# First attention of a three-stage kernel: masks added by quarters of the array, routing products padded to the whole array, first w1 loaded in four steps

## The chip, the cores and the metric

The kernel runs on one core of a Trainium2 chip. The metric is the device time of one execution in microseconds. Each execution works on the whole input: four batches of 576 tokens.

## The reference, cut to what matters

Three layers follow one another: an attention with fixed masks, a mixture of eight experts with one expert per token, and a mixture of four attention experts with two per token.

```
def _attn_ref(q, k, v):                      # q, k, v: (4, 8, 576, 64)
    scores = scale * q @ k.T
    rel = pos[:, None] - pos[None, :]
    mask_local = (rel >= 0) & (rel < 32)                     # heads 0 to 3
    mask_strided = (rel >= 0) & (pos[None, :] % 32 == pos[:, None] % 32)   # heads 4 to 7
    scores = where(mask, scores, -1e9); softmax; @ v
def _moe_ref(x, w_gate, w_local, w1, w2):    # 8 experts, D 512, F 1024
    for each batch b, token s in order:
        fresh = argmax(logits[b, s])
        e = fresh if s == 0 or sigmoid(x @ w_local) < 0.5 else previous token's e
        out[b, s] = softmax(logits)[e] * (relu(x @ w1[e]) @ w2[e])
def _moe2_ref(x, ...):                       # 4 experts, each a causal attention, the top 2 added
```

The output is the third layer's, (4, 576, 512) in float32. The change touches the first layer and the choice of the expert (the routing) in the second.

## The kernel before, in words

The program has one instruction list per engine, and the first about 125 us of it are the first attention. That attention is cut into 16 units, four to a batch: units 0 and 1 of a batch (`u < LOC`) hold two heads each with the local mask, units 2 and 3 two heads each with the strided mask. A unit goes through these functions: `prep` (L342) turns q and k around with transposes on PE, ScalarE (ACT) moves them out of PSUM; `s_mm` (L369 to L393) makes the scores in the PSUM tile `s`, of which there is one; `et` (L405, L409, L416) transposes the weights after the exponential; `pv` (L428, L447) multiplies by v; POOL's queue writes the result to memory (`xd`); `xt` (L469, L472, L476) transposes it again for the routing.

In `s_mm` the mask comes first: for each of the two heads `h` one product of a 128x128 identity in bf16 (`idb`) with a table of zeros and -1e30 (`ml` for local, `ms` for strided) writes the bank of that head with 384, 480 or 288 columns (L369). The scores are then added to it by products that use a quarter of the array each: rows 64h to 64h+63 by the head, columns 64g to 64g+63 by the half of the output's partitions (L374 for local, 64x96; L382 for strided, 36x36, whose outputs start at partitions 0 and 64).

```
for h in range(2):
    nc.tensor.matmul(p[:, h, :nb * w], idb, m, start=True, stop=False, skip_group_check=True)
```

The routing of a batch is a chain of small steps between the units: `logits` (L490), `route0`, `route1` (L507, L508: two transposes that give the logits by token, the second of 32 rows), `route_w`, `route2` (L546: two products with the five columns of `r_key` as the weights), `route2b` (L555, L556: two products with the five rows of `r_row`), `route3` (L571 to L578: ranks, the last product with the one row of `bump`), `route3b` (L613, L619), `route_r`, `route4` (L636: the slots of the tokens).

The order of the work is written out by hand. Each function call is an event with a time; the list is sorted by time and then called in the order of the table `ORD` (309 events). PE runs in exactly the order of the calls (`manual_schedule`); for the other engines the scheduler of the framework places the instructions, so their order also depends on the calls. All loads stand in one queue, SyncE's (SP), in order; a load whose buffer is still read waits there, and so does everything behind it.

Beside the attention the first expert is made ready. `load_w1(0)` is one event that issues four loads of 512 KB (L162) into four buffers called `w1raw`; `split_w1` (16 events, called from `ORD`) splits each buffer in four parts into a rounded part on ACT (L118, `w1h`) and a rest on VectorE (DVE, L119, `w1l`). `load_w2e` (L176) then takes the same four buffers for `w2`, and `split_w2e` splits that. After about 125 us come `xt_early`, `h_early` and `y_early` (expert 0 on the rows of the first three batches), then experts 1 to 7 with their weights streaming in, then the third layer from about 400 us.

Before the units PE does 24 products with zeros (`warm`, L714).

Of the kernel before, what the change touches and what calls it, by code (L numbers as in the profile page):

```python
# [11 lines left out]
BF = mybir.dt.bfloat16  # L12
I32 = mybir.dt.int32
AF = mybir.ActivationFunctionType
OP = mybir.AluOpType
# [17 lines left out]
ORD = [5, 2, 0, 4, 7, 1, 3, 8, 10, 6, 11, 16, 12, 22, 19, 14, 20, 13, 17, 9, 18, 21, 24, 25, 26, 23, 29, 27, 15, 31,  # L33
# [12 lines left out]
NORM = [[[0, 1], [0, 0]], [[1, 0], [0, 0]], [[0, 1], [0, 0]], [[0, 1], [0, 0]], [[0, 0], [1, 1]]]  # L46
# [10 lines left out]
def kernel(  # L57
# [100 lines left out]

    def load_w1(e):
        for c in range(4):  # L160
            t = wpool.tile([128, F], FT, name="w1raw", bufs=4)
            nc.sync.dma_start(t, moe_w1[e, c * 128:(c + 1) * 128, :])  # L162
            RAW1[e, c] = t
# [95 lines left out]
    es = [slot(3, [128, 2, 4, 128], FT, "es0"), ak.tile([128, 2, 5, 128], FT, name="es1")]  # L259
    ml = ac.tile([128, 6, 96], BF)  # L260
    ms = ac.tile([128, 8, 36], BF)
# [8 lines left out]
    for x in kl:  # L270
        nc.vector.memset(x[:, :32], 0.0)
    nc.vector.tensor_copy(ml, ml1[:, None, :].to_broadcast([128, 6, 96]))
    nc.vector.memset(ml[:64, 1, :32], NEG)
    for x in vl:
# [87 lines left out]
    def s_mm(n):  # L362
        b, u = divmod(n, NU)
        loc = u < LOC
        nb, w = (4 + u, 96) if loc else (8, 36)
        p = pa.tile([128, 2, 512], FT, name="s", tag="s", bufs=1)
        m = (ml[:, 1 - u:5] if loc else ms).rearrange("p c k -> p (c k)")
        for h in range(2):
            nc.tensor.matmul(p[:, h, :nb * w], idb, m, start=True, stop=False, skip_group_check=True)  # L369
        if loc:  # L370
            for c, g, a, t in tiles(u):
                for h in range(2):
                    r = slice(64 * h, 64 * h + 64)
# [125 lines left out]
    slot_acc = ac.tile([128, RC, 6, NE], FT)  # L499
    bump = cst.tile([1, NE], BF)  # L500
    lim = cst.tile([128, 2], FT)
    nc.vector.memset(bump, 0.0)

    def route1(b):
        lg = lgs[b % 2]
        p = bank([128, NC5, 32], "lgt")
        nc.tensor.transpose(p[:, :4].rearrange("p g e -> p (g e)"), lts[:, :128], idf)  # L507
        nc.tensor.transpose(p[:, 4], lts[:32, 128:], idf[:32, :32])  # L508
        nc.vector.tensor_copy(lg, p[:, :, :9])
        l8 = lg[:, :, 1:]  # L510
# [10 lines left out]
        nc.vector.scalar_tensor_tensor(fr, lg[:, :, 0], ZC, first, op0=OP.is_lt, op1=OP.max)  # L521
        key = rt.tile([128, 2, NC5], BF, name="r_key", bufs=1)
        nc.vector.tensor_tensor(key[:, 0], m8, fr, op=OP.mult)
        nc.vector.tensor_scalar(key[:, 1], fr, -1.0, 1.0, op0=OP.mult, op1=OP.add)
        ex = rt.tile([128, NC5, NE], FT, name="r_ex", bufs=1)
        nc.vector.tensor_tensor(ex, l8, mxb, op=OP.subtract)
        nc.scalar.activation(ex, ex, AF.Exp)
        RT[b] = key
        EX[b] = ex
# [11 lines left out]
    def route2(b):  # L541
        key = RT[b]
        row = rt.tile([NC5, 128], BF, name="r_row", bufs=1)
        p = bank([NC5, 2, 128], "kr")
        for n in (1, 0):
            nc.tensor.matmul(p[:, n], key[:, n], idb, start=True, stop=True)  # L546
        nf = rt.tile([NC5, 128], FT, name="r_nf", bufs=1)
        nc.scalar.activation(nf, p[:, 1], AF.Copy)
        nc.vector.tensor_tensor_scan(row, nf, p[:, 0], 0.0, op0=OP.mult, op1=OP.add)
        RT[b] = row  # L550

    def route2b(b):
        row = RT.pop(b)
        p = bank([128, 2, NC5], "pk")
        nc.tensor.matmul(p[:, 0], row, idb[:NC5, :NC5], start=True, stop=True)  # L555
        nc.tensor.matmul(p[:, 1], row[:, 127:].to_broadcast([NC5, 128]), idb[:NC5, :NC5], start=True, stop=True)  # L556
        un = rt.tile([128, 2, NC5], FT, name="r_un", bufs=1)
        nc.vector.tensor_scalar(un[:, 0], p[:, 1], 0.0, None, op0=OP.is_equal)
        nc.vector.tensor_tensor_scan(carry[:, 1:], un[:, 0], p[:, 1], 0.0, op0=OP.mult, op1=OP.add)
        nc.vector.scalar_tensor_tensor(un[:, 1], p[:, 0], 0.0, carry[:, :NC5], op0=OP.is_equal, op1=OP.mult)  # L560
        pk = rt.tile([128, NC5], FT, name="r_pk", bufs=1)
        nc.vector.tensor_tensor(pk, un[:, 1], p[:, 0], op=OP.add)
        PK[b] = pk

    def route3(b):
# [11 lines left out]
        if b:  # L577
            nc.tensor.matmul(pr, ones_b[:1], bump[:1, None, :].to_broadcast([1, NC5, NE]), start=False, stop=True,  # L578
                             skip_group_check=True)
# [30 lines left out]
    def route3b(b):  # L610
# [5 lines left out]
        if b == B - 2:  # L616

            pn = bank([1, 1], "pn")
            nc.tensor.matmul(pn, ones_b[:, :1], ohs[:, :1], start=True, stop=True)  # L619
            bm = rt.tile([1, 1], FT, name="r_bm", bufs=1)  # L620
            nc.vector.tensor_scalar(bm, pn, -1.0, float(EARLY), op0=OP.mult, op1=OP.add)
            nc.vector.tensor_scalar(bump[:, :1], bm, 0.0, None, op0=OP.max)

# [59 lines left out]
    def count():  # L683
        p = bank([128, NE], "cnt")
        nc.tensor.matmul(p, ones_b, ohs, start=True, stop=False, skip_group_check=True)
        nc.tensor.matmul(p, ones_b[:1], bump, start=False, stop=True, skip_group_check=True)
        nc.vector.tensor_copy(ext, p)
# [58 lines left out]
    for b in range(B):  # L746
# [4 lines left out]
        ev += [(o + x, *y) for x, y in zip(t, r)]  # L751
    ev += [(SL[0], slots, (slice(0, 2), slice(0, 1), lambda: gather(0, [0, 1], (B - 1) * S))), (6, load_w1, (0,))]
    for c in range(4):
# [698 lines left out]
```

## Time and profile before, and how to read it

| what | us |
|---|---|
| three timed executions | 586.32, 593.21, 592.51 |
| their median | 592.51 |
| the profiled execution, whole | 586.57 |
| its span (first to last instruction) | 584.8 |

The profile comes from one execution. It names engines: PE is the matrix engine, PEld its weight loads, DVE VectorE, ACT ScalarE, POOL GpSimd, SP SyncE; SPq is the queue of loads. A line such as L369 is a line of the kernel before. In the timeline each row is a run of equal instructions: the start in us from the span's start, the time from the first's start to the last's end, the engine and line, what is written from what, the weights' rows and columns (128*128), the moving operand, and the count. Brackets give the idle time ahead of it and what ended it; "issue" stands where the profile shows nothing that the engine waited for. The shares of the DMA are of 16 engines; q8 and q14 of the DMA queues bring instructions.

### The profile page before, as it was taken

To read this page: it belongs to the slowest core of one execution; us is meant where nothing else is said; L and a number is where in the kernel's file an instruction comes from. 1 tells how busy PE (TensorE), PEld (TensorE's weight loads), DVE (VectorE), ACT (ScalarE), POOL (GpSimd) and SP (SyncE) were. 2 spreads that over 40 slices of the span, in tenths; PEclk is the share of its full clock that TensorE was granted. 3 is DMA by queue.
4 is the path that set the end of the run, shared out by engine and by line. 5 is a ranking of instruction groups with operands and counts; after the bars stand their busy time and mean duration, and the time that the engine had idled before them with its cause. 6 is when DMAs were issued, how large, how long until landed. Compare 5 with 4: busy or idle time off the path is not lost. (4 is left out here: it accounts for less than half of the span.)

```text
span 584.8 us, 14159 instructions
## 1 busy us (share of the span) xinstructions
PE 554.6 (95%) x5217; PEld 478.5 (82%) x5217; DVE 383.4 (66%) x1138; ACT 345.9 (59%) x864; POOL 148.8 (25%) x239
## 2 busy tenths in 40 slices
PE   7889899969999999999999999998999999999996
PEld 3778687758779898988989987797987998889864
DVE  2446789855583646474747476158998889898891
ACT  2466775741274544564646567345877876776882
POOL 8232313250422432423343443220000001000000
PEclk9699899989999999999999999999999999999999
DMA  9999989640485765275747360325003402301302
GB/s 182 185 223 217 266 205 218 209 151 1 132 302 191 224 211 167 87 218 192 259 132 251 132 203 28 102 78 129 26 19 71 157 2 58 96 20 41 114 20 90
DMA packets 81127, 82.01 MB, mean 140 GB/s; under 512 B 56840, under 2 KB 57096, under 8 KB 80528
## 3 DMA queue, kind: packets, MB, share of 16 engines
q1 hardware_dynamic: 72768, 64.92, 40.2%
q0 software_dynamic: 8112, 15.76, 8.4%
q8 instruction: 59, 0.97, 0.7%
q14 instruction: 28, 0.23, 0.1%
q10 hardware_dynamic: 160, 0.13, 0.1%
HBM read 61.89 MB, written 21.76 MB: 143 GB/s over the span
## 5 line engine op out<-in xcount | busy, mean ns | idle before, releaser
L196 POOL DMA_INDIRECT yd<-y,sidx x47 | 51.2, 1089 | 91.5 <-ACT y L971 54.3
L1272 ACT ACTIVATE E<-cs,c_mx 128x288 f32<-128x288 f32 (+4 forms) x96 | 45.8, 482 | 13.7 <-DVE c_mx L1270 6.5
L122 PE MATMUL yp<-w2h,h 128*128 128x512 f32 x128 | 51.1, 399 | 0.1
L124 PE MATMUL yp<-w2h,h 128*128 128x512 f32 x128 | 49.9, 390 | 0.0
L123 PE MATMUL yp<-w2l,h 128*128 128x512 f32 x128 | 49.9, 390 | 0.0
L119 DVE TENSOR_TENSOR w1l<-w1raw,w1h 128x1024 fp32r<-128x1024 f32 (+1 forms) x44 | 41.5, 981 | 12.6 <-ACT w1h L118 12.6
L119 DVE TENSOR_TENSOR w2l<-w2raw,w2h 128x512 fp32r<-128x512 f32 x56 | 35.7, 686 | 19.3 <-ACT w2h L118 18.8
L1302 POOL MEMSET E<- 128x128 f32 x40 | 8.3, 211 | 145.7 <-PE cet L1321 68.6
L118 ACT ACTIVATE w1h<-w1raw 128x1024 fp32r<-128x1024 f32 (+1 forms) x44 | 33.9, 837 | 18.6 <-PE hp L123 18.6
L118 ACT ACTIVATE w2h<-w2raw 128x512 fp32r<-128x512 f32 x56 | 31.8, 631 | 18.9 <-PE yp L124 8.2
L705 DVE SCALAR_TENSOR_TENSOR h<-hp,h 128x384 fp32r<-128x384 f32 x48 | 24.8, 552 | 27.2 <-ACT h L704 27.0
L1265 PE MATMUL cs<-qkt 128*128 128x288 f32 (+4 forms) x192 | 39.1, 319 | 0.4 <-DVE qkt L1195 0.4
L1270 DVE TENSOR_REDUCE c_mx<-cs 128x1 f32<-128x288 f32 (+4 forms) x80 | 37.8, 484 | 1.7 <-PE cs L1265 1.0
L122 PE MATMUL qkp<-y,cw 128*128 128x288 f32 x128 | 38.7, 303 | 0.0
L124 PE MATMUL qkp<-y,cw 128*128 128x288 f32 x128 | 37.7, 295 | 0.0
L123 PE MATMUL qkp<-y,cw 128*128 128x288 f32 x128 | 37.7, 294 | 0.0
L704 ACT ACTIVATE h<-hp 128x384 fp32r<-128x384 f32 x48 | 21.4, 490 | 19.6 <-PE hp L124 19.5
L190 POOL DMA_INDIRECT xg<-xd,gidx x24 | 25.1, 1047 | 27.9 <-DVE gidx L648 20.9
L122 PE MATMUL hp<-xo,w1h 128*128 128x320 f32 (+2 forms) x96 | 30.4, 317 | 0.1
L1316 PE MATMUL cet<-idf,E 128*128 128x128 f32 x160 | 28.2, 278 | 2.4 <-ACT et L115 0.8
L123 PE MATMUL hp<-xo,w1h 128*128 128x320 f32 (+2 forms) x96 | 30.1, 314 | 0.0
L124 PE MATMUL hp<-xo,w1l 128*128 128x320 f32 (+2 forms) x96 | 30.1, 314 | 0.0
(371 smaller groups left out, 1683.8 us busy)
## 6 DMA issues: line engine op xcount, KB each, us to landing
w1raw<-in_moe_w_dram SPq DMA_DIRECT2D x32, 512.0 KB
w2raw<-in_moe_w_dram SPq DMA_DIRECT2D x56, 256.0 KB
qkt<-qkt SPq DMA_DIRECT2D x8, 576.0 KB
yr<-yd SPq DMA_DIRECT2D x16, 256.0 KB
out_dram<-co SPq DMA_DIRECT2D x16, 256.0 KB
raw<-in_q_dram SPq DMA_DIRECT2D x16, 144.0 KB
raw<-in_k_dram SPq DMA_DIRECT2D x16, 144.0 KB
raw<-in_q_dram SPq DMA_DIRECT2D x8, 288.0 KB
```

What stands on the lines that cost most here:

```text
L118: nc.scalar.activation(hi, src, AF.Copy)
L119: (eng or nc.vector).tensor_tensor(lo, src, hi.bitcast(FT), op=OP.subtract)
L122: nc.tensor.matmul(o, ah, bh, start=start, stop=False, **kw)
L123: nc.tensor.matmul(o, ah, bl, start=False, stop=False, **kw)
L124: nc.tensor.matmul(o, al, bh, start=False, stop=stop, **kw)
L190: nc.gpsimd.indirect_dma_start(out=t, out_offset=None, in_=xd[:rows], in_offset=bass.IndirectOffsetOnAxis(ap=gidx[:, r, e:e + 1], axis=0))
L196: nc.gpsimd.indirect_dma_start(out=yds[n], out_offset=bass.IndirectOffsetOnAxis(ap=ix(n), axis=0), in_=y, in_offset=None, bounds_check=yds ...
L705: nc.vector.scalar_tensor_tensor(lo, p, 0.0, hi.bitcast(FT), op0=OP.max, op1=OP.subtract)
L1265: nc.tensor.matmul(o[:, h - h0], T[:, h, q0:q0 + 128], T[:, 2 + 2 * x + h, k0:k1], start=x == 0, stop=x == 1, skip_group_check=True)
L1270: nc.vector.tensor_reduce(mx[:, n, h0:h0 + G], o, axis=AX.X, op=OP.max, negate=True)
L1272: nc.scalar.activation(E[:, h, k0:k1], o[:, h - h0], AF.Exp, bias=mx[:, n, h:h + 1], accum_out=sm[:, n, h:h + 1])
L1316: nc.tensor.transpose(p[:, kt * 128:kt * 128 + 128], E[:, kt * 128:kt * 128 + 128], idf)
```

## The change

Three things, and the order table that goes with them. First, `s_mm` adds each mask by four products instead of two: identity rows and columns 64 by 64, rows by the head, columns by the half of the output's partitions, which are the quarters that the score products use; the table of the local mask becomes one block longer (`ml` 7 instead of 6 blocks, 128x672), so that both halves of the partitions can take their own window of it. Second, the routing's small products get whole operands: the second transposition of the logits takes 128 rows of `lts` instead of 32, `key` and `row` become fixed tiles of 128 columns and 128 rows that POOL clears once, `bump` has 128 rows, `pn` 128 outputs. Third, `load_w1(0)` is four events, one for each 512 KB, each with its own place in `ORD`.

```
 def load_w1(e):  ->  def load_w1(e, cs=range(4)):   # for c in cs
-    ml = ac.tile([128, 6, 96], BF)
+    ml = ac.tile([128, 7, 96], BF)
-    nc.vector.memset(ml[:64, 1, :32], NEG)
+    nc.vector.memset(ml[:, 1, :32], NEG)
-        m = (ml[:, 1 - u:5] if loc else ms).rearrange("p c k -> p (c k)")
         for h in range(2):
-            nc.tensor.matmul(p[:, h, :nb * w], idb, m, start=True, stop=False, skip_group_check=True)
+            r = slice(64 * h, 64 * h + 64)
+            for g in range(2):
+                m = (ml[r, 2:6 + u] if g else ml[r, 1 - u:5]) if loc else ms[r]
+                nc.tensor.matmul(p[64 * g:64 * g + 64, h, :nb * w], idb[r, r], m.rearrange("p c k -> p (c k)"),
+                                 start=True, stop=False, skip_group_check=True)
-    bump = cst.tile([1, NE], BF)
+    bump = cst.tile([128, NE], BF)
+    key = ac.tile([128, 2, 128], BF)
+    row = ac.tile([128, 128], BF)
+    nc.gpsimd.memset(key, 0.0)
+    nc.gpsimd.memset(row, 0.0)
-        nc.tensor.transpose(p[:, 4], lts[:32, 128:], idf[:32, :32])
+        nc.tensor.transpose(p[:, 4:].rearrange("p g e -> p (g e)"), lts[:, 128:], idf)
-        nc.tensor.matmul(p[:, 0], row, idb[:NC5, :NC5], start=True, stop=True)
+        nc.tensor.matmul(p[:, 0], row, idb[:, :NC5], start=True, stop=True)
-            nc.tensor.matmul(pr, ones_b[:1], bump[:1, None, :].to_broadcast([1, NC5, NE]), ...
+            nc.tensor.matmul(pr, ones_b, bump[:, None, :].to_broadcast([128, NC5, NE]), ...
-            pn = bank([1, 1], "pn")
+            pn = bank([128, 1], "pn")
-    ev += [..., (6, load_w1, (0,))]
+    ev += [(6 + c * .01, load_w1, (0, (c,))) for c in range(4)]
-    63, 64, 48, 67, 65, 37, 35, 36, 77, 74, 72, 69, 70, 49, 71, 55, 66, 78, 81, 62, 61, 83, 84, 87, 68, 95, 90, 73,
+    63, 64, 48, 67, 65, 37, 35, 36, 77, 74, 72, 69, 70, 49, 71, 55, 66, 78, 81, 62, 61, 83, 84, 87, 68, 98, 93, 73,
...
```

On PE, in the routing of the third batch and the first strided unit behind it (`lgt` is the routing's transposition, `s` the scores' tile, `ms` the strided mask, `kr` the product with the key), before:

```order
566 L507 MATMUL lgt<-idf,lts 128x128
567 L508 MATMUL lgt<-idf,lts 128x32
568 L369 LDWEIGHTS idb
569 L369 MATMUL s<-ms,idb 128x288
570 L369 LDWEIGHTS idb
571 L369 MATMUL s<-ms,idb 128x288
572 L382 MATMUL s<-ks_122,qs_120 36x36 x32
573 L546 LDWEIGHTS r_key
574 L546 MATMUL kr<-idb,r_key 5x128
```

And the same place of the changed kernel on PE:

```order
622 L514 MATMUL lgt<-idf,lts 128x128
623 L515 MATMUL lgt<-idf,lts 128x128
624 L371 LDWEIGHTS idb
625 L371 MATMUL s<-ms,idb 64x288
626 L371 LDWEIGHTS idb
627 L371 MATMUL s<-ms,idb 64x288
628 L371 LDWEIGHTS idb
629 L371 MATMUL s<-ms,idb 64x288
630 L371 LDWEIGHTS idb
631 L371 MATMUL s<-ms,idb 64x288
632 L385 MATMUL s<-ks_122,qs_120 36x36 x32
633 L549 LDWEIGHTS key
```

Nothing changes places on PE; two mask products become four, and each is as long as before.

In SP's queue, where the first expert's w1 is loaded (the loads of q and k are `raw`, those of v are `vla`, `vlb`, `vl` for the local and `vs` for the strided heads), the difference:

```order
 L230 DMA raw_102<-in_k_dram 72x2x512
-L162 DMA w1raw<-in_moe_w_dram 128x1024 x4
+L162 DMA w1raw<-in_moe_w_dram 128x1024
 L240 DMA vla<-in_v_dram 64x4x64
 L240 DMA vlb<-in_v_dram 96x4x64
...
 L240 DMA vlb<-in_v_dram 96x4x64
+L162 DMA w1raw<-in_moe_w_dram 128x1024
 L228 DMA raw_100<-in_q_dram 96x6x64 x2
 L228 DMA raw_100<-in_k_dram 96x6x64 x2
```

One chunk stays where four were; the second stands behind the nine loads of v that follow, the third and fourth further behind, among the loads of the fourth batch.

On ACT, where w1 is split, before and then after:

```order
73 L353 ACTIVATE qs_120<-prep 128x288
74 L118 ACTIVATE w1h<-w1raw 128x256 x8
75 L353 ACTIVATE qs_120<-prep 128x288
76 L115 ACTIVATE ess<-et 128x400
77 L115 ACTIVATE kl_119<-prep 128x288
78 L353 ACTIVATE ql_117<-prep 128x288
79 L118 ACTIVATE w1h<-w1raw 128x256
```

```order
84 L115 ACTIVATE xT_128<-xt 128x512
85 L115 ACTIVATE xT_129<-xt 128x8x36
86 L115 ACTIVATE es_132<-et 96x512
87 L118 ACTIVATE w1h<-w1raw 128x256 x4
88 L115 ACTIVATE xT_129<-xt 128x8x36
89 L115 ACTIVATE ks_123<-prep 128x288
90 L115 ACTIVATE xT_129<-xt 128x8x36
91 L115 ACTIVATE es_132<-et 96x512
92 L396 ACTIVATE z_127<-z_127 128x960
```

At row 74 four splits remain of the eight, and the second chunk's four stand at row 87, where before the last six of the sixteen stood.

## Rows read from the trace of the kernel before

**Rows 1.** The page, busy time of the engines and the granted clock in 40 slices.

```profile
PE 554.6 (95%) x5217; PEld 478.5 (82%) x5217; DVE 383.4 (66%) x1138; ACT 345.9 (59%) x864; POOL 148.8 (25%) x239
PEclk9699899989999999999999999999999999999999
```

**Rows 2.** Stages: busy PE, PEld, DVE, ACT, POOL (count each), clock, DMA share, GB/s.

```profile
0.00:125.00 125.00, 109.84 (x2333) 87.85 (x2333) 82.01 (x257) 75.10 (x179) 48.53 (x104) 0.95 0.87 208
...
250.00:400.00 150.00, 149.13 (x899) 132.07 (x899) 82.63 (x143) 81.27 (x145) 51.55 (x53) 1.00 0.49 157
```

**Rows 3.** Timeline of PE, 58 to 69 us.

```profile
59.05 0.34 PE L447 MATMUL pv<-vs,ess 64*64 64x65 f32 x7
61.65 0.57 PE L447 MATMUL pv<-vs,ess 64*36 64x65 f32 x25 [2.25 <-issue]
62.15 1.23 PE L342 MATMUL prep<-idf,raw 96*128 96x96 f32 x14
```

**Rows 4.** Timeline of PE around 38 and 102 us.

```profile
37.84 0.31 PE L447 MATMUL pv<-vs,ess 64*64 64x65 f32 x4 [1.04 <-issue]
...
102.23 0.41 PE L490 MATMUL lg<-xT,wg 128*32 128x128 f32 x5 [0.68 <-issue]
```

**Rows 5.** PE's products counted between those waits (columns: busy, count, clock, DMA).

```profile
37.83:61.64 23.81, 21.55 (x505) 1.00 0.90 221
61.64:102.22 40.58, 39.08 (x888) 0.96 0.92 226
```

**Rows 6.** DMA queues, 52.5 to 58.5 us, then the instruction queue, 58.5 to 61.5 us.

```profile
q1 hardware_dynamic: 697, 1.33, 84.4%
q0 software_dynamic: 79, 0.26, 12.3%
q14 instruction: 1, 0.01, 0.3%
...
q8 instruction: 1, 0.02, 2.7%
```

**Rows 7.** PE in two stretches of low clock (columns: busy, count, clock, DMA).

```profile
16.00:26.10 10.10, 8.89 (x108) 0.50 1.02 176
63.70:67.10 3.40, 3.40 (x65) 0.50 1.07 266
```

**Rows 8.** Timeline of SP's queue.

```profile
52.74 2.74 SPq L162 DMA_DIRECT2D w1raw<-in_moe_w_dram  x4
...
68.22 0.48 SPq L240 DMA_DIRECT2D vlb<-in_v_dram  x1
...
91.27 1.32 SPq L176 DMA_DIRECT2D w2e<-in_moe_w_dram  x1
```

**Rows 9.** Timeline of ACT, 63 to 99 us.

```profile
63.86 2.56 ACT L118 ACTIVATE w1h<-w1raw 128x256 fp32r<-128x256 f32 x8
...
72.83 1.97 ACT L118 ACTIVATE w1h<-w1raw 128x256 fp32r<-128x256 f32 x6
...
98.24 1.15 ACT L118 ACTIVATE w2s<-w2e 128x512 fp32r<-128x512 f32 x2 [1.33 <-DMA w2e<-in_moe_w_dram]
```

**Rows 10.** Timeline of PE around three units' masks.

```profile
96.30 0.57 PE L369 MATMUL s<-ml,idb 128*128 128x480 bf16 x2
96.80 1.21 PE L374 MATMUL s<-kl,ql 64*64 64x96 f32 x40
...
107.08 0.27 PE L507 MATMUL lgt<-idf,lts 128*128 128x128 f32 x1
107.28 0.24 PE L508 MATMUL lgt<-idf,lts 32*128 32x32 f32 x1
107.46 0.42 PE L369 MATMUL s<-ms,idb 128*128 128x288 bf16 x2
107.81 0.79 PE L382 MATMUL s<-ks,qs 64*36 64x36 f32 x64
...
114.03 0.69 PE L447 MATMUL pv<-vs,ess 64*64 64x65 f32 x32
```

More of the change, by code (lines that the diff above doesn't have):

```diff
@@ L157, with load_w1 @@
     RAW1, RAW2, W1, W2 = {}, {}, {}, {}
-    def load_w1(e):
-        for c in range(4):
+    def load_w1(e, cs=range(4)):
+        for c in cs:
             t = wpool.tile([128, F], FT, name="w1raw", bufs=4)
@@ L271 @@
         nc.vector.memset(x[:, :32], 0.0)
-    nc.vector.tensor_copy(ml, ml1[:, None, :].to_broadcast([128, 6, 96]))
-    nc.vector.memset(ml[:64, 1, :32], NEG)
+    nc.vector.tensor_copy(ml, ml1[:, None, :].to_broadcast([128, 7, 96]))
+    nc.vector.memset(ml[:, 1, :32], NEG)
     for x in vl:
@@ L499 @@
     slot_acc = ac.tile([128, RC, 6, NE], FT)
-    bump = cst.tile([1, NE], BF)
+    bump = cst.tile([128, NE], BF)
+    key = ac.tile([128, 2, 128], BF)
+    row = ac.tile([128, 128], BF)
     lim = cst.tile([128, 2], FT)
     nc.vector.memset(bump, 0.0)
+    nc.gpsimd.memset(key, 0.0)
+    nc.gpsimd.memset(row, 0.0)
     def route1(b):
         lg = lgs[b % 2]
-        p = bank([128, NC5, 32], "lgt")
+        p = bank([128, 8, 32], "lgt")
         nc.tensor.transpose(p[:, :4].rearrange("p g e -> p (g e)"), lts[:, :128], idf)
-        nc.tensor.transpose(p[:, 4], lts[:32, 128:], idf[:32, :32])
-        nc.vector.tensor_copy(lg, p[:, :, :9])
+        nc.tensor.transpose(p[:, 4:].rearrange("p g e -> p (g e)"), lts[:, 128:], idf)
+        nc.vector.tensor_copy(lg, p[:, :NC5, :9])
         l8 = lg[:, :, 1:]
@@ L521, in route1 @@
         nc.vector.scalar_tensor_tensor(fr, lg[:, :, 0], ZC, first, op0=OP.is_lt, op1=OP.max)
-        key = rt.tile([128, 2, NC5], BF, name="r_key", bufs=1)
-        nc.vector.tensor_tensor(key[:, 0], m8, fr, op=OP.mult)
-        nc.vector.tensor_scalar(key[:, 1], fr, -1.0, 1.0, op0=OP.mult, op1=OP.add)
+        nc.vector.tensor_tensor(key[:, 0, :NC5], m8, fr, op=OP.mult)
+        nc.vector.tensor_scalar(key[:, 1, :NC5], fr, -1.0, 1.0, op0=OP.mult, op1=OP.add)
         ex = rt.tile([128, NC5, NE], FT, name="r_ex", bufs=1)
@@ L527, in route1 @@
         nc.scalar.activation(ex, ex, AF.Exp)
-        RT[b] = key
         EX[b] = ex
@@ L541, in route2 @@
     def route2(b):
-        key = RT[b]
-        row = rt.tile([NC5, 128], BF, name="r_row", bufs=1)
-        p = bank([NC5, 2, 128], "kr")
+        p = bank([128, 2, 128], "kr")
         for n in (1, 0):
@@ L547, in route2 @@
         nf = rt.tile([NC5, 128], FT, name="r_nf", bufs=1)
-        nc.scalar.activation(nf, p[:, 1], AF.Copy)
-        nc.vector.tensor_tensor_scan(row, nf, p[:, 0], 0.0, op0=OP.mult, op1=OP.add)
-        RT[b] = row
+        nc.scalar.activation(nf, p[:NC5, 1], AF.Copy)
+        nc.vector.tensor_tensor_scan(row[:NC5], nf, p[:NC5, 0], 0.0, op0=OP.mult, op1=OP.add)
     def route2b(b):
-        row = RT.pop(b)
         p = bank([128, 2, NC5], "pk")
-        nc.tensor.matmul(p[:, 0], row, idb[:NC5, :NC5], start=True, stop=True)
-        nc.tensor.matmul(p[:, 1], row[:, 127:].to_broadcast([NC5, 128]), idb[:NC5, :NC5], start=True, stop=True)
+        nc.tensor.matmul(p[:, 0], row, idb[:, :NC5], start=True, stop=True)
+        nc.tensor.matmul(p[:, 1], row[:, 127:].to_broadcast([128, 128]), idb[:, :NC5], start=True, stop=True)
         un = rt.tile([128, 2, NC5], FT, name="r_un", bufs=1)
@@ L577, in route3 @@
         if b:
-            nc.tensor.matmul(pr, ones_b[:1], bump[:1, None, :].to_broadcast([1, NC5, NE]), start=False, stop=True,
+            nc.tensor.matmul(pr, ones_b, bump[:, None, :].to_broadcast([128, NC5, NE]), start=False, stop=True,
                              skip_group_check=True)
@@ L616, in route3b @@
         if b == B - 2:
-            pn = bank([1, 1], "pn")
-            nc.tensor.matmul(pn, ones_b[:, :1], ohs[:, :1], start=True, stop=True)
+            pn = bank([128, 1], "pn")
+            nc.tensor.matmul(pn, ones_b, ohs[:, :1], start=True, stop=True)
             bm = rt.tile([1, 1], FT, name="r_bm", bufs=1)
-            nc.vector.tensor_scalar(bm, pn, -1.0, float(EARLY), op0=OP.mult, op1=OP.add)
-            nc.vector.tensor_scalar(bump[:, :1], bm, 0.0, None, op0=OP.max)
+            nc.vector.tensor_scalar(bm, pn[:1], -1.0, float(EARLY), op0=OP.mult, op1=OP.add)
+            nc.vector.tensor_scalar(bump[:1, :1], bm, 0.0, None, op0=OP.max)
     def route_r(b):
@@ L685, in count @@
         nc.tensor.matmul(p, ones_b, ohs, start=True, stop=False, skip_group_check=True)
-        nc.tensor.matmul(p, ones_b[:1], bump, start=False, stop=True, skip_group_check=True)
+        nc.tensor.matmul(p, ones_b, bump, start=False, stop=True, skip_group_check=True)
         nc.vector.tensor_copy(ext, p)
@@ L751 @@
         ev += [(o + x, *y) for x, y in zip(t, r)]
-    ev += [(SL[0], slots, (slice(0, 2), slice(0, 1), lambda: gather(0, [0, 1], (B - 1) * S))), (6, load_w1, (0,))]
+    ev += [(SL[0], slots, (slice(0, 2), slice(0, 1), lambda: gather(0, [0, 1], (B - 1) * S)))]
+    ev += [(6 + c * .01, load_w1, (0, (c,))) for c in range(4)]
     for c in range(4):
```

22 rows, old and new, of the table ORD are left out of this document.

## Prediction

> **What bounds the kernel now.** I read the page first: PE is busy 95% of the span, and its clock row shows where the matrix engine ran slower [rows 1]. The table by stage then says where PE sets the time and where it doesn't [rows 2]. From 250 to 400 us PE is busy 149.13 of 150 us, so what the first stage gains is passed on to the end, as long as the weights behind it come in time. From 0 to 125 us PE is busy 109.84 of 125 at a clock of 0.95, and the DMA engines are at 0.87 of their time. So this stage is bound by PE and transfers together, with ACT and DVE at 60 to 66%: a cut on PE is worth something in it, but not all of it.
>
> Where PE stands still there, the timeline tells more than the totals. The longest wait in the middle of the stage is 2.25 us before 61.65 us: seven of 32 products of one `pv` had run, the other 25 followed later, and the profile names no releaser ("issue") [rows 3]. Two more waits have the same look, 1.04 and 0.68 us, each inside a run of equal products [rows 4]. Between them PE ran 505 and 888 products [rows 5], a ratio of 1 to 1.76, or 4 to 7.03: the waits stand at whole multiples of one length of PE's program, which is what a program that arrives in equal pieces would show. The DMA queues show such pieces: the instruction queue q8 brought nothing from 52.5 to 58.5 us, while 1.33 MB of data went through q1, and one packet after 58.5 us [rows 6]. The four w1 loads, 2 MB together, were issued from 52.74 to 55.48 us [rows 8]. I read this as PE waiting for its own instructions behind w1. That is an inference: no row says what a wait named "issue" waits for.
>
> The wait had a second price. The granted clock was 0.50, the 1.2 GHz level, from 63.7 to 67.1 us, and PE was busy all of these 3.40 us [rows 7]; at 2.4 GHz the same work would take about half, so some 1.7 us went there. The other low stretch, 16.0 to 26.1 us, follows waits on the first loads and is not touched.
>
> **The masks.** Each of the 16 units has two full products, and after the change four on quarters, with as many columns each. From the mask's start to the first score's start it is 0.50 us for 480 columns (96.30 to 96.80) and 0.35 us for 288 (107.46 to 107.81) [rows 10]. The difference, 0.15 us over 2 x 192 columns, gives 0.39 ns a column, which fits 2.4 GHz, and leaves some 0.12 us that doesn't depend on the columns; I put that down to the change between the whole array and quarters, and it isn't saved, only moved ahead of the masks. What the four cost depends on how far quarters run at once. The nearest row is `pv` at L447, with the same order of quarters: 32 products of 65 columns in 0.69 us, 22 ns each [rows 10]. The transposes, also float32, take 1.23 us for 14 of 96 columns, or 0.91 ns a column [rows 3]; at that rate 32 products in turn would take 1.9 us, so about 2.7 ran at once. With 2.5 at once, four masks take 4 x 288 x 0.39 / 2.5 = 180 ns instead of 225 ns, and 240 instead of 300 for 384 columns, 300 instead of 374 for 480. Over 8, 4 and 4 units that is 0.36 + 0.24 + 0.30 = 0.9 us, and 1.0 with the units that run at the low clock. Bounds: all four at once save half, 8 x 0.112 + 4 x 0.150 + 4 x 0.187 = 2.2 us; one after another they add twice that, 4.5 us. I take the value by the `pv` row: -1.0.
>
> There is a rule against it. The Trainium skill (TensorE: Matmul & The Clock Gate, Part 3, What overlaps and what doesn't) says that weight loads overlap running products only where the rows of the array differ; here each head's two products share their rows and stand side by side, so by the rule two could run at once, and the masks would save nothing, 1.0 us less than my sum. The `pv` row has the same neighbours and shows more than two at once, if my rate for float32 holds.
>
> **The routing.** The narrow second transposition, 32 rows, stands 0.18 us before the mask behind it, and the two together take 0.38 us (107.08 to 107.46) [rows 10]. Two whole ones in a row at 0.91 ns a column are 0.23 us: 0.15 us saved, four times 0.6. The products with `key`, `row` and `bump` have no row of the padded kind; by the same pair I allow 0.1 us either way for each, three times in four batches, 1.2 us. Much of this chain waits for DVE, so I take -0.5, bounds -1.8 and +0.6. POOL's two clearings come once, in front of the units, beside the first loads, and cost nothing there; uncovered they would be two short instructions.
>
> **w1 in four steps.** At 52.74 us SP now issues 512 KB, a quarter, before the v loads. If the instruction packet was late because of the other 1.5 MB, the wait of 2.25 us goes, and with it the 1.7 us of low clock: 3.95 us at most. The transfers that follow are no fewer, and a stage with its DMA at 0.87 gives some of it back as other late loads; I keep three quarters, -3.0.
>
> The change also adds a wait. ACT takes its instructions in order. Before, it took the first eight splits at 63.86 us and the last six at 72.83 us, and none waited for data [rows 9]. Now the second chunk's four splits stand where the six did, and its load stands behind the v loads, the last of which was issued at 68.22 us and took 0.48 [rows 8]. How long 512 KB takes to land is shown by w2e: issued at 91.27 us, it released ACT at 98.24 us, 7.0 us later [rows 8, 9]. So the second chunk lands near 68.7 + 7.0 = 75.7 us, against 72.8 us when ACT gets there, and earlier still by up to 1.9 us, as six splits of 0.32 us (2.56 / 8) no longer stand ahead. The wait is 2.9 to 4.8 us if the DMA is as crowded as at 91 us, and nothing if it is free of the 1.5 MB moved. Behind it in ACT's queue are the evictions of the routing's transposes (`xT`), of k, and the next weights (`es`), and PE needs their banks of PSUM and their results. Four banks give PE some slack. I take 2 us of wait on ACT and +1.5 on the path; bounds 0 and +5.5, the latter 4.8 plus part of a second such wait at a later chunk. For the whole edit that is -1.5, between -3.95 and +5.5.
>
> **The sum.** -1.0 - 0.5 - 3.0 + 1.5 = -3.0 us. The profiled execution took 586.57 us, so the same execution would take 583.6. It lies 5.9 us below the median of the three timed ones, 592.51; one of them, 586.32, lies where it does. I forecast the median: 592.5 - 3.0 = 589.5 us.
>
> **The rivals.**
> *The fetch wait doesn't go, or stands elsewhere.* For it: the other two waits of this look, at 37.84 and 102.23 us, stand where no w1 load is under way [rows 4, 8], so other traffic makes them too; and the added instructions shift each later piece's edge. Against it: they are 1.04 and 0.68 us, under half of the one behind w1. Then the masks and the routing alone count: 592.5 - 1.5 = 591.0.
> *ACT's wait for the second chunk takes over.* It decides from about 5 us of wait on the path upward. Priced: 4.8 us at the chunk, 1.7 us of low clock as after the wait of 61.65 us, and 1.5 us at a later chunk make 8.0; against -1.0, -0.5 and -3.95 the kernel is slower by 2.5, 595.0. For it: the row of w2e, and no spare row between load and split. Against it: SP's queue runs ahead as soon as PE frees buffers earlier, and the DMA carries 1.5 MB less in that stretch.
> *The quarters run in turn.* Masks +4.5, routing -0.5, w1 -1.5: slower by 2.5 as well, 595.0. Against it: the 22 ns of the `pv` row.
> *The whole w1 gain arrives.* Masks -2.2, routing -0.5, w1 -3.95 without a wait: -6.6, 585.9.
>
> **How the numbers follow.** Forecast 0.42, fetch wait stays 0.2, ACT's wait 0.18, quarters in turn 0.08, the whole gain 0.12. The range also has to hold either level of the timed executions, 586 or 593, since the median of a few runs can fall on either: 586.3 - 3.0 = 583.3 at the lower one, and a little for the whole gain; 595.0 and a little above for the two slow rivals. That gives 582.5 to 596.0. Two per cent, 11.8 us, is about what a measurement of this kernel can tell from no change. Faster by more would take most of PE's 15 us of idle time before 125 us; slower by more would take two of the slow cases together. So 0.03, 0.92, 0.05.
>
> **What would show it right or wrong.** Right: no "issue" wait over 1 us near 60 us and the clock at 1.00 from 63 to 68 us; 0.30 us from first mask to first score for 288 columns, instead of 0.35; 125 us reached about 3 us earlier. Wrong: ACT's first `w1h` of the second chunk waiting for a load over 4 us with PE idle behind it; masks of 288 columns over 0.5 us; a new wait named "issue" of 2 us; or an early stage that gains while a later wait, for gathered rows or weights, takes it back.

## The result, and the profile after

| | before | after |
|---|---|---|
| median of the timed executions, us | 587.81 (22 executions, 583.18 to 593.21) | 593.76 (22 executions, 588.50 to 597.01) |
| ratio to before, 95% interval | | 1.0099 (1.0075 to 1.0123) |
| the profiled execution, whole, us | 586.57 | 590.39 |
| its span, us | 584.8 | 588.6 |

The changed kernel is slower by 1.0%, some 5.9 us of 588; the forecast was 3.0 us faster. The time is inside the range, the sign is wrong. (The prediction counted from 592.5 us, the median of three executions; that of 22 is 587.8.) The ratios here leave out executions more than 1.5% above the fastest of their kernel, so they can differ a little from the quotient of the medians. The profiled execution of after shows 3.8 us of this in its span, and the first stage has all of it: the gathered rows of the second batch are turned around (`xpe`, the stage's last step before the experts) 4.7 us later. PE's timeline there, before:

```profile
128.14 0.73 PE L666 MATMUL xpe<-idf,xg 128*128 128x128 f32 x4 [2.10 <-DMA xg<-xd,gidx]
```

and after:

```profile
132.84 1.09 PE L667 MATMUL xpe<-idf,xg 128*128 128x128 f32 x4 [2.34 <-DMA xg<-xd,gidx]
```

The page of after, busy times and clock, which answers to [rows 1]:

```profile
PE 552.9 (94%) x5246; PEld 481.4 (82%) x5249; DVE 384.0 (65%) x1138; ACT 347.1 (59%) x864; POOL 152.3 (26%) x241
PEclk9789798998999999999999999999999999999999
```

The stages of after, which answer to [rows 2]:

```profile
0.00:125.00 125.00, 105.41 (x2273) 88.16 (x2276) 79.63 (x251) 73.68 (x175) 44.55 (x101) 0.92 0.85 201
250.00:400.00 150.00, 148.60 (x884) 131.17 (x886) 82.87 (x134) 82.54 (x147) 53.68 (x53) 1.00 0.49 157
```

PE's busy time fell by 1.7 us over the span, and yet the kernel takes longer. In the first 125 us PE was busy 4.4 us less (105.41 against 109.84) at a clock of 0.92 instead of 0.95, and had run 60 products fewer, with the added masks counted. PE waits more there and runs slower; the late stage is as full as it was. Where it waits is seen in ten-microsecond windows of PE (busy, count, clock, share of the DMA), first of before:

```profile
60.00:70.00 10.00, 8.36 (x168) 0.83 1.04 299
90.00:100.00 10.00, 9.81 (x232) 1.00 1.02 216
```

and the same of after:

```profile
60.00:70.00 10.00, 9.26 (x155) 0.66 1.15 265
90.00:100.00 10.00, 7.22 (x148) 0.93 0.97 240
```

From 90 to 100 us PE lost 2.6 us of work, from 60 to 70 us it was busy but at a lower clock. ACT's timeline says what happened from 90 us on:

```profile
92.59 0.67 ACT L115 ACTIVATE xT<-xt 128x288 f32<-128x288 f32 x1
95.58 0.42 ACT L118 ACTIVATE w1h<-w1raw 128x256 fp32r<-128x256 f32 x1 [2.32 <-DMA w1raw<-in_moe_w_dram]
95.90 0.58 ACT L115 ACTIVATE xT<-xt 128x512 f32<-128x512 f32 x1
96.38 0.83 ACT L396 ACTIVATE z<-z 128x768 f32<-128x768 f32 x1
```

and PE's says who stood behind it:

```profile
97.26 0.64 PE L408 MATMUL et<-idf,z 128*96 128x128 f32 x4 [2.66 <-ACT z L396]
```

The masks of the fourth batch's two local units show where the time went. The first unit's start 0.96 us later than before, those of the second, behind PE's wait, 4.23 us later (96.30 us in [rows 10], now 100.53). Before:

```profile
89.39 0.50 PE L369 MATMUL s<-ml,idb 128*128 128x384 bf16 x2
```

and after:

```profile
90.35 0.36 PE L371 MATMUL s<-ml,idb 64*64 64x384 bf16 x4
...
100.53 0.61 PE L371 MATMUL s<-ml,idb 64*64 64x480 bf16 x4
```

ACT came to the first split of the fourth chunk and stood 2.32 us, until the load had landed. The exponential of the next scores (`z`, L396) is two places behind that split in ACT's queue, and PE stood 2.66 us before the transposes that read it. The three chunks before were taken without a wait ahead of them, at 65.54, 73.41 and 85.92 us. The loads of the four, in SP's queue:

```profile
53.44 0.71 SPq L162 DMA_DIRECT2D w1raw<-in_moe_w_dram  x1
...
64.20 0.48 SPq L162 DMA_DIRECT2D w1raw<-in_moe_w_dram  x1
...
78.21 0.56 SPq L162 DMA_DIRECT2D w1raw<-in_moe_w_dram  x1
...
89.76 0.60 SPq L162 DMA_DIRECT2D w1raw<-in_moe_w_dram  x1
...
95.57 0.46 SPq L230 DMA_DIRECT2D raw<-in_k_dram  x1
```

Issue to landing of the fourth: from 89.76 to about 95.5 us, 5.8 us. The last load of k (L230) now goes out at 95.57 us; before it went at 90.31 us. So the attention's own loads moved back too.

The waits named "issue" [rows 3, 4] did not go:

```profile
36.82 0.42 PE L450 MATMUL pv<-vs,ess 64*64 64x65 f32 x12 [1.93 <-issue]
...
60.74 0.22 PE L385 MATMUL s<-ks,qs 64*36 64x36 f32 x1 [2.51 <-issue]
```

PE ran 506 products between these two; before it was 505 [rows 5]. The wait stands at the same distance in PE's program, with 512 KB of w1 ahead of it instead of 2 MB. Only that of 102.23 us has no counterpart in after.

The masks and the second routing transposition, which answer to [rows 10]:

```profile
110.45 0.33 PE L514 MATMUL lgt<-idf,lts 128*128 128x128 f32 x1
110.62 0.27 PE L515 MATMUL lgt<-idf,lts 128*128 128x128 f32 x1
110.82 0.32 PE L371 MATMUL s<-ms,idb 64*64 64x288 bf16 x4
110.97 0.76 PE L385 MATMUL s<-ks,qs 64*36 64x36 f32 x64
...
73.07 0.41 PE L371 MATMUL s<-ml,idb 64*64 64x480 bf16 x4
73.27 1.03 PE L377 MATMUL s<-kl,ql 64*64 64x96 f32 x40
```

From first mask to first score it is 0.15 us for 288 columns instead of 0.35, and 0.20 for 480 instead of 0.50. The prediction had 0.30 for the first. So the masks did save on PE, more than forecast, and the kernel was slower all the same. Not all of what the first score gains is saved, though: behind a product of the whole array a quarter mask starts later than a whole one did. From the second transposition (whole in both) to the mask it is 0.20 us here (110.62 to 110.82), and 0.11 in the kernel with the routing alone, whose masks are whole:

```profile
106.84 0.27 PE L511 MATMUL lgt<-idf,lts 128*128 128x128 f32 x1
106.95 0.27 PE L512 MATMUL lgt<-idf,lts 128*128 128x128 f32 x1
107.06 0.41 PE L369 MATMUL s<-ms,idb 128*128 128x288 bf16 x2
107.40 0.79 PE L382 MATMUL s<-ks,qs 64*36 64x36 f32 x64
```

### The profile page after: what moved, and what is told of

It is laid out like the page before. It is cut to its first block, busy times and chain, and to the rows that moved or that the text cites. A ratio compares the mean times of both kernels' runs of the same rounds, so it can differ in the third digit from the quotient of the medians.

```text
span 588.6 us, 14217 instructions
## 1 busy us (share of the span) xinstructions
PE 552.9 (94%) x5246; PEld 481.4 (82%) x5249; DVE 384.0 (65%) x1138; ACT 347.1 (59%) x864; POOL 152.3 (26%) x241
## 5 line engine op out<-in xcount | busy, mean ns | idle before, releaser
L196 POOL DMA_INDIRECT yd<-y,sidx x47 | 53.6, 1140 | 88.5 <-ACT y L973 51.4
```

The source lines that it names most:

```text
L196: nc.gpsimd.indirect_dma_start(out=yds[n], out_offset=bass.IndirectOffsetOnAxis(ap=ix(n), axis=0), in_=y, in_offset=None, bounds_check=yds ...
```

## The experiments

Two theories were set against each other first. Theory A: loading w1 in four steps costs more than it gives, by ACT's wait for the fourth chunk and by loads that come later. Theory B: the masks by quarters let PE's clock drop, and so cost more than they save. Theory A was later divided: is it the wait on ACT, or (A2) the attention's own later loads? Every kernel was timed in twelve executions beside the kernel before; "clock" is the mean granted clock over the executions that the ratio uses (before: 0.983 beside the first four kernels, 0.982 beside the others; the change: 0.973).

| kernel | median us | ratio to before | 95% interval | clock |
|---|---|---|---|---|
| masks alone | 588.28 | 0.9983 | 0.9944 to 1.0023 | 0.979 |
| routing alone | 586.81 | 0.9991 | 0.9956 to 1.0025 | 0.982 |
| w1 in steps alone | 594.37 | 1.0107 | 1.0069 to 1.0146 | 0.977 |
| masks and routing | 585.15 | 0.9965 | 0.9929 to 1.0000 | 0.979 |
| the change, chunks 3 and 4 sooner | 586.69 | 0.9959 | 0.9932 to 0.9986 | 0.979 |
| the change, no wait for chunk 4 | 589.94 | 1.0006 | 0.9981 to 1.0031 | 0.976 |
| masks and routing, both forms of mask | 586.63 | 0.9968 | 0.9951 to 0.9986 | 0.985 |
| the change, w1 in one place, later | 587.65 | 0.9982 | 0.9956 to 1.0009 | 0.979 |
| masks and routing, quarters three times | 588.43 | 0.9991 | 0.9965 to 1.0017 | 0.981 |
| chunks 3 and 4 sooner, both forms of mask | 589.64 | 0.9997 | 0.9960 to 1.0033 | 0.982 |
| chunks 3 and 4 sooner, old masks | 586.69 | 0.9968 | 0.9938 to 0.9998 | 0.979 |

**Each part by itself.** The kernel before with one part of the change, and with two.

Masks alone:

```
-            nc.tensor.matmul(p[:, h, :nb * w], idb, m, start=True, ...)
+            for g in range(2):
+                nc.tensor.matmul(p[64 * g:64 * g + 64, h, :nb * w], idb[r, r], m..., start=True, ...)
```

> The masks by quarters alone, order table and loads as before. Theory A (the loss of 5.9 us comes from w1 in four steps: ACT stands 2.3 us at the fourth chunk, and the loads of the last units leave later): no loss here, 584 to 588 us against 587.8, since the start-to-score time falls from 0.35 to 0.15 us for 288 columns, about 3.7 us over the 16 units. Theory B (with less work of the whole array the clock stands longer at 1.2 GHz): 590 to 594 us, and more than three stretches of 0.50 before 135 us.

Routing alone:

```
-        nc.tensor.transpose(p[:, 4], lts[:32, 128:], idf[:32, :32])
+        nc.tensor.transpose(p[:, 4:].rearrange("p g e -> p (g e)"), lts[:, 128:], idf)
...
```

> The routing's products padded alone, order table and loads as before. Theory A and theory B alike: within 1.5 us of the kernel before, 586 to 589 us. Only if the order of DVE and ACT, which shifts by some 15 rows with it, matters by itself would it be over 590.

w1 alone, with the order table that belongs to it:

```
-    ev += [..., (6, load_w1, (0,))]
+    ev += [(6 + c * .01, load_w1, (0, (c,))) for c in range(4)]
```

> The four w1 loads and the new order table alone; PE's program is that of the kernel before row by row. Theory A: 591 to 596 us, with ACT waiting about 2 us for the fourth chunk and PE behind it. Theory B: 586 to 589 us. The wait named issue near 60 us stays at about 2 us if it has nothing to do with the bulk of w1, and goes if it has.

Masks and routing, the change with w1 undone:

```
-    ev += [(6 + c * .01, load_w1, (0, (c,))) for c in range(4)]
+    ev += [..., (6, load_w1, (0,))]
```

> The changed kernel with its four w1 loads put back into one event and the old order table: PE's program is that of the changed kernel. Theory A: 584 to 588 us. Theory B: 590 to 595 us. If the wait named issue stands at multiples of 256 instructions of PE's program, it comes at the same instructions as in the changed kernel.

w1 in steps alone gives 1.0107, the whole loss of the change (1.0099); masks and routing together give 0.9965. Theory A holds, theory B doesn't: the masks alone are not slower. They are hardly faster either, and the clock may have a share in that. The masks alone ran at a mean clock of 0.979 against 0.983. In their profiled execution the wait named "issue" near 60 us came at the same product as in the change, longer:

```profile
61.75 0.27 PE L385 MATMUL s<-ks,qs 64*36 64x36 f32 x1 [4.58 <-issue]
```

and the windows behind it (busy, count, clock, share of the DMA) show the lower level of 1.2 GHz for nearly all of 60 to 70 us and for some of the next ten, where before the first had 0.83 and the next was at 1.00:

```profile
60.00:70.00 10.00, 8.25 (x130) 0.52 1.03 285
70.00:80.00 10.00, 9.12 (x178) 0.79 0.60 140
```

The profiled execution of w1 alone is the fastest of its twelve, 586.46 us where their median is 594.37, so it doesn't show the loss. ACT's waits for w1 are shorter in it than in the change, 0.71 us for the third chunk and 0.76 for the fourth:

```profile
92.31 0.42 ACT L118 ACTIVATE w1h<-w1raw 128x256 fp32r<-128x256 f32 x1 [0.76 <-DMA w1raw<-in_moe_w_dram]
```

It also shows what stands behind the "issue" wait when that is short:

```profile
59.48 0.57 PE L447 MATMUL pv<-vs,ess 64*36 64x65 f32 x25 [0.38 <-issue]
59.98 0.47 PE L342 MATMUL prep<-idf,raw 96*128 96x96 f32 x3
61.53 0.94 PE L342 MATMUL prep<-idf,raw 72*128 72x72 f32 x11 [1.08 <-DMA raw<-in_k_dram]
```

PE came past the "issue" wait 2.2 us earlier than in the profile of before [rows 3], only to stand before the next transposes, whose k had not landed. It got to them at 61.53 us. Before, the 14 transposes (the same 3 and 11 in one row) began at 62.15 us, so at 1.23 us for 14 the 11 began near 62.4. Of the 2.2 us about 0.9 was left.

**What of w1 costs.** The change with the third load beside the second and the fourth where the third stood:

```
-    ... 110, 89, 119, 94 ... 139, 128, 90, 165 ... 208, 179, 91, 198 ...
+    ... 110, 89, 90, 119, 94 ... 139, 128, 91, 165 ... 208, 179, 198 ...
```

> The changed kernel with its four w1 loads issued sooner: the third beside the second, the fourth where the third stood; nothing else moved by hand. Theory A (the fourth chunk lands 2.3 us too late and ACT stands before its split, with the exponentials and TensorE behind it): no wait of over 0.5 us for w1raw on ACT, and most of the 5.9 us come back, 585 to 589 us, near the 585.2 of masks and routing without the steps. Theory A2 (what costs is that loads between the chunks' loads, raw and vs, come later, whatever ACT waits): still 592 or more, since these loads stay behind w1 or move further back. Theory B (the quarter masks alone let the clock drop): 593 as the change.

The change with ACT's wait for the fourth chunk taken out, the loads and PE's products in the order of the change:

```
-            split(h[:, s], l[:, s], RAW1[e, c][:, s])
+            split(h[:, s], l[:, s], RAW1[e, 2 if (e, c) == (0, 3) else c][:, s])
```

> The changed kernel, but the four splits of expert 0's fourth w1 chunk read the third chunk's buffer (the fourth chunk's data is left out of the computation; its load is still issued, in its place). The order of SP's loads and of TensorE's instructions is that of the change. Theory A (ACT's wait for the fourth chunk): the wait of 2.3 us on ACT and the 2.7 us of TensorE behind it are gone, and 588 to 590 us come out. Theory A2 (later loads of the attention itself): 592 to 594 us, with the waits on ACT gone all the same.

With the two loads sooner the ratio is 0.9959: all of the loss is gone, and the kernel is faster than before by 0.1 to 0.7%. ACT still waits once for a chunk, 0.92 us instead of 2.32, and PE's wait behind `z` is 0.49 us instead of 2.66:

```profile
87.76 1.34 ACT L106 ACTIVATE w1h<-w1raw 128x256 fp32r<-128x256 f32 x4 [0.92 <-DMA w1raw<-in_moe_w_dram]
```

```profile
96.89 0.64 PE L396 MATMUL et<-idf,z 128*96 128x128 f32 x4 [0.49 <-ACT z L384]
```

The expectation had said that no wait for w1raw on ACT would be over 0.5 us; there was one of 0.92, at a point where less hung on it. With the wait taken out and the loads left where the change has them, the ratio is 1.0006. PE's row there:

```profile
100.61 0.64 PE L408 MATMUL et<-idf,z 128*96 128x128 f32 x4 [0.50 <-ACT z L396]
```

So of the change's 0.99% ACT's wait has about 0.93% or 5.5 us (0.4 to 1.4% by the ends of the two intervals), by far the most. Two things limit this. The scheduler placed the splits anew: the fourth chunk's four now stand directly behind the third's, and no longer two places ahead of `z`, so what went is the wait together with that place:

```profile
90.33 2.55 ACT L118 ACTIVATE w1h<-w1raw 128x256 fp32r<-128x256 f32 x8
```

And the profiled execution of this kernel, 594.69 us, is the second longest of its twelve: it shows which wait is gone, not the time. From 1.0006 to 0.9959 some 0.47% or 2.8 us remain. That kernel still has its loads in the later order, as A2 would have it, but its interval and that of the kernel with the loads sooner overlap narrowly (0.9981 to 0.9986), and the splits' places differ as well: A2 may have a share, which is not shown.

**Does w1 make the "issue" wait?** The change with the four loads in one place again, fourteen events later:

```
-    ... 93, 73, 88, 79 ... 115, 120, 97 ... 110, 89, 119 ... 128, 90, 165 ... 179, 91, 198 ...
+    ... 93, 73, 79 ... 115, 120, 88, 89, 90, 91, 97 ... 110, 119 ... 128, 165 ... 179, 198 ...
```

> The changed kernel with all four w1 loads in one place again, but 14 steps of the order later, behind about 60 us, so that nothing of w1 is on the queues when TensorE's instruction packet of 58 to 60 us is fetched. If the w1 load delays that packet (step 'w1 in four steps' of the prediction): the wait marked issue near 60 us is under 0.5 us, and the time is 583 or less unless the chunks now come late for ACT. If the packet is late for another reason (the loads of q, k and v ahead of it): the wait is 2 us or more as in the kernels with w1 ahead of it, and the time is 585 to 588.

The loads went out from 60.79 us on, and there is no wait named "issue" near 60 us. In its place stands this:

```profile
62.92 0.95 PE L330 MATMUL prep<-idf,raw 72*128 72x72 f32 x11 [1.02 <-DMA raw<-in_k_dram]
```

The time was 587.65, not under 583, although ACT waited for no chunk of w1; a wait named "issue" of 1.36 us stands at 90.74 us instead. With nothing of w1 ahead of it the wait near 60 us was gone in this one profile. With one chunk ahead it was 0.38 (w1 alone), 0.72 (loads sooner, both forms of mask), 1.05 (old masks), 1.42 (loads sooner), 2.51 (the change) and 3.10 us (no wait for chunk 4). With all four it was 2.23, 2.25, 3.82 and 4.58 us (masks and routing, before, routing alone, masks alone), but with both forms of mask there was none, and with the quarters three times 0.49 us, at 66.18 us. (More masks on PE shift the place of these waits in its program.) So it is not shown that w1 in front makes the wait or lengthens it: these are single profiles, and the groups overlap. The other half shows more often: of the six kernels with a wait near 60 us of about 1 us at most, or with none, five have PE standing 0.8 to 3.0 us before the same 11 transposes for their k. The sixth, loads sooner with both forms of mask, has no such wait. The kernel with both forms of mask shows it as well, with all of w1 ahead:

```profile
60.98 0.95 PE L342 MATMUL prep<-idf,raw 72*128 72x72 f32 x11 [3.02 <-DMA raw<-in_k_dram]
```

**What the loads in steps are worth, well placed.** The kernel with the loads sooner, but masks as before:

```
-            for g in range(2):
-                nc.tensor.matmul(p[64 * g:64 * g + 64, h, :nb * w], idb[r, r], m..., start=True, ...)
+            nc.tensor.matmul(p[:, h, :nb * w], idb, m, start=True, ...)
```

> Routing as changed, w1 in four steps with the third and fourth load issued sooner, and the masks as before: what loading in steps is worth by itself where no chunk comes late. If steps well placed gain what the prediction kept of the fetch wait (3.0 us less 0.5 for routing): 585 us or less, clock 0.985 or above. If the steps gain nothing and only their lateness costs: 587 to 589 us with the clock of the kernel before, 0.982.

586.69 us, ratio 0.9968. Beside routing alone, 0.9991, that is 1.4 us less, within the intervals of both; with the quarter masks in, the steps give 0.9959 where w1 in one place gives 0.9965. So well-placed steps are worth 0 to 1.4 us. The clock was 0.979, not 0.985: no step in the clock came back.

**What the masks are worth, and the clock.** Three kernels add mask products to PE again. Masks and routing, w1 as before, with the old masks in front of the quarters, which overwrite them:

```
+            nc.tensor.matmul(p[:, h, :nb * w], idb, (ml[:, 1 - u:5] if loc else ms)..., start=True, stop=True, ...)
+        for h in range(2):
             r = slice(64 * h, 64 * h + 64)
```

> Masks and routing as changed, w1 as before, and in front of the quarter masks the old masks over the whole array as well, which the quarters then overwrite: some 5.8 us more TensorE work (0.35 to 0.50 us at each of 16 score tiles), by the first mask to first score times of the kernel before. If only the work counts: 585.2 + 5.8 = 591 us. If the masks over the whole array keep the clock up (mean granted clock 0.982 with them, 0.979 without them): the mean clock is back at 0.982 or above, and the time is 588 to 589, less than the added work.

The same without the old masks, the quarters written three times:

```
-        for h in range(2):
+        for h in (0, 1) * 3:
             r = slice(64 * h, 64 * h + 64)
```

> Masks and routing as changed, w1 as before, with the quarter masks written three times instead of once: about as much TensorE time added as by the old masks in front of the quarters, but none of it over the whole array. If what the shorter masks cost in clock comes from the work dropped, the mean granted clock is 0.984 or above, as with both forms (0.985), and the time stays near 586.5. If it comes from working in quarters, the clock stays at 0.979 or falls, and the added work is paid in full: 589 to 591 us.

And the two that had gained by themselves in one kernel, w1's loads sooner and both forms of mask (the edit is that of the first of these three):

> The changed kernel with the third and fourth w1 load issued sooner, and the old masks over the whole array written in front of the quarter masks. If the two effects add (ratio 0.9959 by the loads, mean clock 0.985 by the masks): clock 0.984 or above and 583 to 586 us, below every kernel so far. If the added masks are paid in full beside w1 in steps: 588 us or more.

The old masks in front of the quarters cost next to nothing: 0.9968 against 0.9965, with the clock at 0.985 against 0.979. Its windows from 60 to 80 us:

```profile
60.00:70.00 10.00, 8.81 (x153) 0.83 1.04 290
70.00:80.00 10.00, 9.39 (x247) 1.00 0.99 210
```

and those of masks and routing, without the old masks:

```profile
60.00:70.00 10.00, 9.94 (x184) 0.70 1.06 287
70.00:80.00 10.00, 8.72 (x241) 1.00 0.98 207
```

Quarters three times added nearly as much and came between: 0.9991 at 0.981. That fits neither end of its expectation. For 480 columns it takes 0.61 us to the first score, against 0.20 with one set of quarters, so each further set of four took 0.20:

```profile
75.06 0.81 PE L371 MATMUL s<-ml,idb 64*64 64x480 bf16 x12
75.67 1.03 PE L377 MATMUL s<-kl,ql 64*64 64x96 f32 x40
```

Then the combination didn't add up: with w1's loads sooner, both forms of mask give 0.9997, 0.4% more than the quarters alone, although its clock is higher (0.982 against 0.979); the two intervals overlap. And the old masks instead of the quarters change neither clock (0.979 in both) nor time much there (0.9968 and 0.9959). So in the other pairs less mask work on PE goes with a lower clock, in this one it doesn't, and the clock alone doesn't order the times. What is measured is that the quarter masks, which take some 2.8 us off PE's own work (worked out below), are worth 0.5 to 1.5 us of the kernel's time: 0.5 with w1's loads sooner, 1.0 by themselves, 1.5 beside the routing (0.9991 against 0.9965). That is less than the intervals can tell from nothing. Why the rest is not seen stays open in part.

The kernel with w1's loads sooner is the best that was found, 0.9959 (0.9932 to 0.9986), better than before and than the change. Masks and routing without the steps stand beside it, within the intervals.

## Why the prediction was wrong, point by point

**What bounds the stage.** Right in kind: PE and transfers together set it, and what it loses is passed on. 4.7 us later at the end of the stage became 3.8 us of span.

**The masks, −1.0.** Near the net, but both steps to it were off. The first that failed is "2.5 at once", from the `pv` row: four masks of 288 columns pass in 0.15 us, where one product of 288 columns at the prediction's 0.39 ns a column takes 0.11, and a further set of four with 480 columns takes 0.20, where one takes 0.19. So nearly all four run at once. The Trainium skill (TensorE: Matmul & The Clock Gate, Part 3, What overlaps and what doesn't) would have had two at once at most; the rows speak against it here. The second step, "it isn't saved, only moved ahead of the masks", holds for 0.09 of the 0.12 us where a whole-array product stands ahead (0.20 against 0.11 us). By that step the sign for 288 columns should have been 0.18 us, not the 0.30 that the prediction gave. Where products on quarters stand ahead, as behind `pv`, nothing is moved, and the way to the mask gets shorter too: from the first of 32 `pv` products to the last unit's mask 0.49 us (118.82 to 119.31) instead of 0.62 (114.03 to 114.65). From first mask to first score the saving is 0.20 us for each of 8 units with 288 columns, 0.30 for each of 4 with 480, and 0.25 taken for the 4 between: 8 x 0.20 + 4 x 0.30 + 4 x 0.25 = 3.8 us. Counted from the product ahead of the masks to the last score, with waits left out, the 16 units of masks and routing take some 2.8 us less than those of routing alone; that is PE's saving, and it too lies beyond the bound of 2.2. The masks alone gained 0.17%, 1.0 us, with an interval of ±2.3, so that the net is right by luck. The step missing from the sum is that PE's work and the kernel's time are two things in a stage where transfers end some of the waits; the prediction had said so of the stage and then booked the masks in full.

**The routing, −0.5.** Right as far as it can be told: −0.09%, ±0.35%. With the routing alone the pair of transposes takes 0.22 us to the mask behind it (106.84 to 107.06) instead of 0.38, which is the 0.15 us that the prediction reckoned. In the change it is 0.37 (110.45 to 110.82), 0.09 of it the later start of the quarter mask.

**w1 in four steps, −1.5.** This is the step that turned the sign: it measured +6.3 us by itself (1.07% of 588). Both of its terms were off.

The kept gain of 3.0 us was not there. The step "If the instruction packet was late because of the other 1.5 MB, the wait of 2.25 us goes" failed twice. In the change the wait was 2.51 us with one chunk in front. And in five of the six kernels where it was short or gone, the load of k for the next transposes ended a wait 0.8 to 3.0 us long at nearly the same time. What the waits named "issue" wait for stays open. The prediction named the wait and its price in clock, but not what is late next behind it. Well-placed steps gained 0 to 1.4 us.

The cost of 1.5 us was put in the wrong place. The arithmetic of issue and 7.0 us to landing was near: the fourth chunk took 5.8. But it was worked out for the second chunk, from 68.7 us on. That chunk went out at 64.20 us, 4.5 us earlier than reckoned, as SP's queue ran ahead, and ACT did not wait for it. The fourth was "a second such wait at a later chunk", and was given no working of its own; ACT stood before it at 93.26 us, 3.5 us after its load was issued, where the landing took 5.8. Nor was its place in ACT's queue asked for: two places ahead of an exponential that PE needs at once. The wait of 2.32 us on ACT became 2.66 on PE, a stretch of low clock behind it (0.50, the 1.2 GHz level, from 99 to 102 us; 1.00 in both windows of before from 90 to 110), and some 5.5 us of the time, twice the length of PE's wait.

**The rivals.** "ACT's wait for the second chunk takes over" had the right sign and mechanism, less than half of the size (slower by 2.5), a chance of 0.18 and the wrong chunk. "The fetch wait doesn't go, or stands elsewhere" came true as well, at the same place in PE's program. The two do not exclude each other, which the prediction's list had them do: with both, its own prices give −1.0 − 0.5 + 4.8 + 1.7 = +5.0, close to the +5.9 measured, but by luck: the wait priced at 4.8 us was 2.3 on ACT and 2.7 on PE. "The quarters run in turn" and "the whole w1 gain arrives" are out.

**The signs to look for.** Of the signs of being right none came: the "issue" wait near 60 us was 2.51 us, the clock from 63 to 68 us 0.51, and the stage ended later. The list of what would show it wrong had a wait on ACT for the second chunk, over 4 us, and 'a new wait named "issue" of 2 us'. The second came only as the old wait, which stayed; the first came at 2.3 us and two chunks later, and was enough.

**The range.** That the measured 593.76 us lies between 582.5 and 596.0 is luck of the base: from the 587.8 us of 22 executions the same sum of −3.0 gives 584.8, and the change measured 9 us more.

## What to carry to other kernels

A load that is broken into steps has as many deadlines as steps: work out issue, landing and first reader for each, the last above all, and look at what stands behind that reader in its engine's queue. Before booking a stall as gain, find what the engine would wait for next if the stall weren't there; here it was another load, due within a microsecond or so of the same time. And where transfers share in bounding a stage, don't book work taken off the busy engine at its own length: some 2.8 us of it were worth 0.5 to 1.5 here.

## What the runs showed of the hardware that was not expected

Four bf16 products on the four quarters of the array, each pair on the same rows, ran almost wholly at once: 4 x 288 columns took 0.15 us to the first score and 4 x 480 took 0.20, where two whole-array products of the same lengths took 0.35 and 0.50; two further sets of 4 x 480 added 0.41. Behind a whole-array product the first of them started 0.09 us later than a whole-array mask did (0.20 against 0.11).

The waits named "issue" keep their distance in PE's program: 505 products between two of them before, 506 after. Near 60 us they stand, where there is one, at the same product in all kernels with the same products on PE: ahead of the last of a group of scores with the quarter masks and inside one `pv` without. The length of those near 60 us varied from 0.38 to 4.58 us from kernel to kernel, while the DMA's share was about 0.9 to 1.1. That they are waits for PE's own program is still an inference.
